# Banded attention and a four-expert layer on one core: dummy products, mask load, weight fetches and the pacing of x operands changed together

## The chip, the cores and the metric

The kernel runs on one core of one Trainium2 chip. The metric is the device time of one execution in microseconds (us). The kernel before has a median of 854.83 us over three runs (854.17 to 855.73).

## The reference, cut to what matters

Everything is float32. Four batches, eight heads, 576 positions, head size 64; then 2304 tokens of width 512, four experts with a hidden width of 1024.

```python
scores = 1/sqrt(64) * q @ k.T                  # per batch and head
mask   = 0 <= rel < 32                         # heads 0..3 (rel = row - column)
mask   = 0 <= rel < 128 and rel % 4 == 0       # heads 4..7
attn   = softmax(where(mask, scores, -1e9)) @ v
x      = attn laid out as [2304, 512]
p      = probs / (sum(probs) + 1e-9)
out    = sum over e of p[:, e] * (relu(x @ w1[e]) @ w2[e])
```

## The kernel before, in words

The host reorders the positions of heads 4 to 7 so that their dilated window becomes a band as well, and pads and transposes q, k and v. On the chip there are two kinds of work.

**Attention** goes by groups of three blocks of 64 queries of one pair of heads: 48 groups, twelve per batch. The first two steps take one group each, every later one two, so there are 25 steps. `attention` (L220) gives eight stages; in iteration n of the loop at L708 stage `s_qk` and `s_max` work on step n, `s_sub` and `s_exp` on step n-1, `s_sum` and `s_norm` on n-2, `s_tr` on n-3 and `s_av` on n-4. TensorE makes the scores (tile `sc`, L264), the transposes (`pt`, L329) and the products with v (`po`, L349); VectorE adds the mask with a running minimum (L278) and sums (L310); GpSimd subtracts and scales (L294, L317); ScalarE takes the exponential (L302) and copies `pt` and `po` out of PSUM (L336, L365). `sc`, `pt` and `po` share four PSUM banks, and an iteration takes five, so the second `sc` of an iteration waits for ScalarE's copy of the same iteration's `po`.

**The experts** run as a generator, `experts` (L500). Every float32 operand is split into a high and a low float32r part, and a product takes three matmuls per 128 rows (`product`, L378). The hidden width is cut into 16 units u, the tokens into three blocks m of 768. A visit (u, m) makes first products of x and w1 (`mm1_a`, L415, and `mm1_b`, L428: seven products in Strassen's manner, two PSUM banks `x` and `y`), then six second products with w2 (`mm2`, L463: each 128 x 512, added into `acc` by VectorE at L488). Block 0 is visited first with every u, blocks 1 and 2 after it; block 0 starts while attention still runs.

**What sets the order.** Each engine works its own list in the order in which the program names the instructions. The loop at L708 issues, per iteration, the loads of q, k and v, the eight stages, some preparations, and then either dummy matmuls (`dummies`, L676: a bfloat16 matmul of 256 columns on a constant, its result read by nobody) or, from START (iteration 10) on, steps of the expert generator: two per iteration up to OPEN (iteration 15), twelve after it (PACE). Preparations (splits of w1, w2 and x, sums of w1 or x quarters) are generators in two lists, `queue` and `later`. `step()` (L569) lets the first of a list do its next piece. After every yield of the experts one piece of `queue` runs, a second if `queue` is longer than 8, and otherwise one of `later` if `queue` is shorter than 5. `later` holds the x operands of blocks 1 and 2 (`x_part`, L208: a ScalarE copy and a subtraction, by VectorE for odd halves i and by GpSimd for even ones; `x_sums`, L198: four VectorE subtractions per half). `need` (L580) runs pieces on the spot until the one wanted is done: at L556 it wants `x_sums` of half 5.

**Loads.** SyncE issues q, k, the mask, the weights and the probabilities; ScalarE issues the v of batches 0 and 1. q, k and v have six buffers each. The program as built deals eight completion counters in turn to the loads of both issuing engines, so a load also waits until the load eight places before it has landed, and what stands behind it on its engine waits with it. The probabilities come in pieces of 16 bytes (L737); w1 and w2 units are 512 KB each.

Of the kernel before, what the change touches and what calls it, by code (L numbers as in the profile page):

```python
# [21 lines left out]
def band_masks(S):  # L22


    import numpy as np

    masks, which = [], []
    for run in (S, S // DILATION):
        for i in range(S // QB):
            a = (i * QB + np.arange(QB))[:, None]  # L30
            c = (i * QB - WINDOW + np.arange(KB))[None, :]
            seen = (c >= 0) & (a - c >= 0) & (a - c < WINDOW) & (a // run == c // run)
            m = np.where(seen, np.float32(0), np.float32(-8e9))
            same = [j for j, other in enumerate(masks) if np.array_equal(other, m)]
            if not same:
                same = [len(masks)]
                masks.append(m)
            which.append(same[0])
    return np.stack(masks), which
# [3 lines left out]
def kernel(  # L43
# [11 lines left out]
    nc = tc.nc  # L55
    _, which = band_masks(qT.shape[3])
    B, NP, _, S = qT.shape
    NT, DM = out.shape
    E, _, F = w1.shape
# [35 lines left out]
    def fetch_w1(u):  # L95
        e, s = divmod(u % NU, FPE)
        r = wp.tile([128, 4, FU], F32, tag="r1", name="r1", bufs=2)
        nc.sync.dma_start(
            out=r, in_=w1[e, :, s * FU:(s + 1) * FU].rearrange("(c p) f -> p c f", p=128)
        )  # L100
        raw1[u] = r

    def fetch_w2(u):
        e, s = divmod(u % NU, FPE)
        r = wp.tile([128, 2, DM], F32, tag="r2", name="r2")
        nc.sync.dma_start(
            out=r, in_=w2[e, s * FU:(s + 1) * FU, :].rearrange("(c p) d -> p c d", p=128)
        )
        raw2[u] = r
# [110 lines left out]
    def attention(ap, xrp, pa):  # L220
        mask = ap.tile(list(masks.shape), F32, name="mask", bufs=1)
# [143 lines left out]
                nc.scalar.activation(out=dst, in_=src, func=AF.Copy)  # L365

        def load_masks():
            nc.sync.dma_start(out=mask, in_=masks)


        stages = (
# [1 line left out]
            (s_qk, 0), (s_max, 0),  # L373
        )
        return chunk, load_masks, load_qk, load_v, stages


# [85 lines left out]
    def mm2(k, first, last, half):  # L463
        u, m = k
        e = u // FPE % E
        if first and m not in acc_t:
            if m == NBL - 1:
                pools["late"]()
            acc_t[m] = pools["acc"].tile([128, TB // 128, DM], F32, name=f"acc_{m}")
        for i in range(TH // 128):  # L470
            at = half * (TH // 128) + i
            tt = m * (TB // 128) + at
            acc = acc_t[m][:, at, :]
            po = pools["m2"].tile([128, 512], F32, tag="m2", name="m2")

            cs = range(2) if half == 0 else (1, 0)
            for n, (c, low) in enumerate([(c, low) for low in range(2) for c in cs]):
                h = h_t[k, f"{c + 1}{half + 1}"][low][:, i * 128:(i + 1) * 128]
                for x, w in enumerate(w2_op[u, c][:2 - low]):
                    nc.tensor.matmul(  # L480
                        po, h, w, start=(n == 0 and x == 0), stop=(n == 3)
                    )
            if first:
                nc.vector.tensor_scalar(
                    out=acc, in0=po, scalar1=pn[:, tt, e:e + 1], scalar2=None, op0=ALU.mult
                )
            else:
                nc.vector.scalar_tensor_tensor(  # L488
                    out=acc, in0=po, scalar=pn[:, tt, e:e + 1], in1=acc,
                    op0=ALU.mult, op1=ALU.add,  # L490
                )
            if last:
                nc.sync.dma_start(out=out[tt * 128:(tt + 1) * 128, :], in_=acc)
            yield


    visits = [(u, 0) for u in range(1, NU)]
# [2 lines left out]
    def experts(begin):  # L500
# [24 lines left out]
        for i, (u, m) in enumerate(visits):  # L525
# [22 lines left out]
            if m == blocks[0]:  # L548
                need(w2_late, u)
            yield from mm2((u, m), *ends, 1)  # L550
            if i + 1 < len(visits):
                begin()
                yield from opening
                if visits[i + 1] == (NU - 1, 0):

                    need(x_sums, 5)  # L556
                    for n in ("T2", "T1"):
                        for j in (4, 5):
                            prepare(x_part, j, n)
            yield from mm2((u, m), *ends, 0)  # L560
            if m == blocks[-1] and u + 2 <= LAST:
                prepare(w2_late, u + 2)
# [3 lines left out]
    queue = []  # L566
    later = []

    def step(of=None):  # L569
        of = queue if of is None else of  # L570
        while of:
            if next(of[0][1], 0) != 0:
                return
            of.pop(0)

    def prepare(what, *args, soon=False, of=None):
        of = queue if of is None else of
        of.insert(0 if soon else len(of), ((what, args), what(*args)))
# [11 lines left out]
    with tc.manual_schedule():  # L590
# [58 lines left out]
        def weigh():  # L649

            nc.vector.reduce_sum(out=ps_, in_=pw, axis=mybir.AxisListType.X)
            nc.vector.tensor_scalar(
                out=ps_, in0=ps_, scalar1=1e-9, scalar2=None, op0=ALU.add
            )
            nc.vector.reciprocal(out=pr_, in_=ps_)
            nc.vector.tensor_tensor(
                out=pn, in0=pw, in1=pr_.to_broadcast([128, NTT, E]), op=ALU.mult
            )
# [17 lines left out]
        def dummies(n):  # L676

            for _ in range(n):
                wt = pools["m2"].tile([128, 512], F32, tag="m2", name="wt")
                nc.tensor.matmul(wt[:, :256], warm[:, :128], warm, start=True, stop=True)  # L680
# [21 lines left out]
        flat = [g for s in steps for g in s]  # L702
        first_x = []
        qk_done = av_done = qk_next = v_next = 0

        dummies(18)
        ffn = experts(begin)
        for n in range(len(steps) + LAG):  # L708
            while qk_next < min(qk_done + min(6, 3 + n), len(flat)):
                load_qk(*flat[qk_next])  # L710
                if qk_next == 0:
                    load_masks()
                qk_next += 1
            while v_next < min(av_done + 6, qk_done + 2, len(flat)):
                load_v(*flat[v_next])
                v_next += 1
            for stage, lag in stages:
                if 0 <= n - lag < len(steps):
                    stage(n - lag, steps[n - lag])
            if n < len(steps):  # L720
                qk_done += len(steps[n])
            if n >= LAG:
                av_done += len(steps[n - LAG])
            for i, names in when.get(n, ()):
                for name in names:
                    of = first_x if i < 2 else later
                    if name is None or name == "T2":
                        prepare(x_sums, i, of=of)
                    if name is not None:
                        prepare(x_part, i, name.upper(), of=of)  # L730
            queue[:0] = first_x
            first_x.clear()
            if n == 3:
                fetch_w1(0)
            if n == 4:
                fetch_w2(0)
                nc.sync.dma_start(out=pw, in_=probs.rearrange("(t p) e -> p t e", p=128))  # L737
            if n == 5:
                prepare(w1_split, 0)
            if n == 7:  # L740
                prepare(w2_late, 0)
                fetch_w1(1)
            if n == START + 1:
                weigh()
                prepare(w1_split, 1)
                prepare(w1_sums, 1)
            if n == OPEN - 1:
                prepare(w2_late, 1)
            if n == START + 2:
                fetch_w2(1)  # L750
            if n == OPEN:
                fetch_w1(2)
            if n == OPEN:
                gate.add("open")
            if n < START:
                dummies(4 if n < 4 else 1)
                step()
                if n > 4:
                    step()
                    step()  # L760
                continue
            for _ in range(PACE if "open" in gate else 2):
                if next(ffn) == "idle":
                    dummies(2)
                    for _ in range(3):
                        step()
                    break
                step()
                if len(queue) > 8:
                    step()  # L770
                elif later and len(queue) < 5:
                    step(later)
        gate.add("over")
        for _ in ffn:
            step()
            if len(queue) > 6:
                step()
            step(later)


# [53 lines left out]
```

## Time and profile before

| what | value |
|---|---|
| median of three runs | 854.83 us |
| the profiled execution | 850.82 us |
| its span, first to last instruction | 849.0 us |
| TensorE busy | 828.1 us, 98% of the span |
| chain that ended last: TensorE's share | 92% |
| VectorE, GpSimd, ScalarE busy | 499.9, 419.1, 327.6 us |
| mean granted TensorE clock | 0.994 |
| loads of k, of v by ScalarE, of the probabilities: issue to landing | 3.3, 4.1, 5.9 us |

The busy times say how long an engine worked in all, not when. Times inside the execution are counted from the first instruction. L numbers are lines of the kernel.

### The profile page before, as it was taken

What the parts mean: (1) busy time and instruction counts of PE and PEld (TensorE: products, weight loads), DVE (VectorE), ACT (ScalarE), POOL (GpSimd) and SP (SyncE); (2) the same over time, 40 slices, a digit from 0 to 9 for tenths busy, and PEclk for the clock granted to TensorE, in tenths of its full rate; (3) what the DMA queues carried; (4) which work ended last, traced back from release to release, by engine and by line L of the source; (5) the groups of instructions that cost most, each with busy time, mean ns of one, the idle gap of its engine ahead of it and who ended that gap; (6) DMA issues with size and microseconds to landing.
All of it is one profiled execution on the core that took longest, in us unless ns stands there. A gap on an engine that the chain in (4) does not pass through costs nothing.

```text
span 849.0 us, 13445 instructions
## 1 busy us (share of the span) xinstructions
PE 828.1 (98%) x5090; PEld 732.1 (86%) x5090; DVE 499.9 (59%) x1027; ACT 327.6 (39%) x772; POOL 419.1 (49%) x484
## 2 busy tenths in 40 slices
PE   8798999999999999999999999999999999999998
PEld 5577788887898888899899898898998998988986
DVE  4777766669555568655545545555555455455554
ACT  3555454445454355533233233242242242232321
POOL 4677987677676678931432332342341342242210
PEclk9999999999999999999999999999999999999999
DMA  8762322332221222310100100101101001010003
GB/s 234 218 184 73 128 85 84 108 120 64 78 90 51 57 71 72 124 51 26 50 25 25 51 26 26 50 25 38 37 26 50 26 25 49 26 35 17 1 26 124
DMA packets 54528, 56.77 MB, mean 67 GB/s; under 512 B 5952, under 2 KB 43840, under 8 KB 54464
## 3 DMA queue, kind: packets, MB, share of 16 engines
q1 hardware_dynamic: 49472, 52.38, 19.9%
q10 hardware_dynamic: 4992, 3.54, 1.5%
q8 instruction: 40, 0.66, 0.3%
q14 instruction: 24, 0.20, 0.1%
HBM read 51.19 MB, written 4.72 MB: 66 GB/s over the span
## 4 chain that ended last, share of the span: by engine, by line
PE 92%; DVE 3%; DMA 1%; ACT 1%; POOL 1%; issue 1%; SPq 0%; ACTq 0%; POOLq 0%; DVEq 0%
PE m L480 45%; PE m1x L382 24%; PE m1y L382 17%; PE po L349 2%; PE sc L264 2%; PE pt L329 2%; DMA q_s<-qT 1%; PE wt L680 1%; DVE acc L488 1%; DMA k_s<-kT 1%; DVE xl_T L116 1%; DVE hl L406 0%; ACT hh L400 0%; DVE xr L203 0%; DVE s L423 0%
## 5 line engine op out<-in xcount | busy, mean ns | idle before, releaser
L488 DVE SCALAR_TENSOR_TENSOR acc<-m,pn,acc 128x512 f32<-128x512 f32 x270 | 201.9, 749 | 130.9 <-PE m L480 130.7
L480 PE MATMUL m<-w2h,hh 128*128 128x512 f32 x576 | 226.9, 394 | 3.9 <-DVE acc L488 3.2
L480 PE MATMUL m<-w2l,hh 128*128 128x512 f32 x576 | 225.4, 391 | 0.0
L116 POOL TENSOR_TENSOR g2l<-r,g2h 128x256 fp32r<-128x256 f32 x124 | 93.0, 775 | 239.7 <-PE m L480 212.2
L480 PE MATMUL m<-w2h,hl 128*128 128x512 f32 x576 | 178.5, 391 | 0.0
L400 ACT ACTIVATE hh<-s 128x384 fp32r<-128x384 f32 x94 | 49.4, 526 | 248.3 <-DVE s L423 197.8
L480 PEld LDWEIGHTS m<-w2h,hh 128*128 128x128 f32 x576 | 108.1, 188 | 26.8 <-DVE acc L488 6.1
L480 PEld LDWEIGHTS m<-w2h,hl 128*128 128x128 f32 x576 | 108.1, 188 | 24.0 <-DVE hl L406 0.3
L480 PEld LDWEIGHTS m<-w2l,hh 128*128 128x128 f32 x576 | 108.2, 188 | 20.1
L116 POOL TENSOR_TENSOR w2l<-r,w2h 128x512 fp32r<-128x512 f32 x62 | 80.6, 1320 | 45.4 <-ACT w2h L113 45.0
L116 POOL TENSOR_TENSOR g1l<-r,g1h 128x256 fp32r<-128x256 f32 x93 | 68.5, 752 | 66.9 <-ACT g1h L113 66.9
L439 DVE TENSOR_TENSOR s<-m1x,s 128x384 f32<-128x384 f32 x47 | 26.2, 557 | 103.0 <-PE m1x L382 101.3
L432 ACT ACTIVATE u<-m1x 128x384 f32<-128x384 f32 x47 | 23.1, 492 | 144.4 <-PE m1x L382 144.4
L406 DVE SCALAR_TENSOR_TENSOR hl<-s,hh 128x384 fp32r<-128x384 f32 x94 | 60.2, 640 | 28.4 <-ACT hh L400 28.4
L382 PE MATMUL m1x<-xh_T,g2h 128*128 128x384 f32 x156 | 53.1, 340 | 1.8 <-DVE s L423 1.8
L382 PE MATMUL m1x<-xl_T,g2h 128*128 128x384 f32 x156 | 52.9, 339 | 0.0
L382 PE MATMUL m1x<-xh_T,g2l 128*128 128x384 f32 x156 | 52.7, 338 | 0.0
L113 ACT ACTIVATE g2h<-r 128x256 fp32r<-128x256 f32 x125 | 43.4, 405 | 4.4 <-POOL r L145 4.4
L382 PE MATMUL m1y<-xl_B,g2h 128*128 128x384 f32 x128 | 43.0, 336 | 0.0
L382 PE MATMUL m1y<-xh_B,g2h 128*128 128x384 f32 x128 | 43.0, 336 | 0.0
L382 PE MATMUL m1y<-xh_B,g2l 128*128 128x384 f32 x128 | 42.9, 335 | 0.0
L278 DVE CUSTOM_DVE_ANT_0 sm<-sc,mask 128x96 f32<-128x96 f32 x144 | 27.8, 254 | 18.8 <-PE sc L264 17.4
(92 smaller groups left out, 1542.3 us busy)
## 6 DMA issues: line engine op xcount, KB each, us to landing
r<-w SPq DMA_DIRECT2D x64, 512.0 KB, 3.5
k_s<-kT SPq DMA_DIRECT2D x48, 112.0 KB, 3.3
q_s<-qT SPq DMA_DIRECT2D x48, 96.0 KB, 3.4
out<-acc SPq DMA_DIRECT2D x18, 256.0 KB, 2.0
v_s<-vw ACTq DMA_DIRECT2D x24, 144.0 KB, 4.1
v_s<-vw SPq DMA_DIRECT2D x24, 144.0 KB, 3.2
mask<-masks SPq DMA_DIRECT2D x1, 288.0 KB, 4.6
pw<-probs SPq DMA_DIRECT2D x1, 36.0 KB, 5.9
```

Of the source, the lines that this page charges most:

```text
L113: nc.scalar.activation(out=hi, in_=src, func=AF.Copy)
L116: lo_eng.tensor_tensor(out=lo, in0=src, in1=hi.bitcast(F32), op=ALU.subtract)
L264: nc.tensor.matmul(banks[swap][o, i * KB:(i + 1) * KB], q_s[h, c0:c0 + QB], k_s[h, c0:c0 + KB], start=True, stop=True, skip_group_check=True,)
L278: nc.vector.tensor_tensor_reduce(out=sm[:, k * GB + i, :KB], in0=banks[k][:, i * KB:(i + 1) * KB], in1=mask[:, which[blk if p < NP // 2 el ...
L329: nc.tensor.transpose(pt[:KB, i * 128:(i + 1) * 128], sm[:, k * GB + i, :KB], ident)
L382: nc.tensor.matmul(bank, w[:, k], x[:, k], start=(first and k == 0 and i == 0), stop=(last and k == 1 and i == 2), skip_group_check=True,)
L400: nc.scalar.activation(out=hi, in_=src, func=AF.Relu)
L406: nc.vector.scalar_tensor_tensor(out=lo, in0=src, scalar=0.0, in1=hi.bitcast(F32), op0=ALU.max, op1=ALU.subtract)
L432: nc.scalar.activation(out=u2, in_=x, func=AF.Copy)
L439: nc.vector.tensor_tensor(out=s5, in0=x, in1=s5, op=ALU.add)
L480: nc.tensor.matmul(po, h, w, start=(n == 0 and x == 0), stop=(n == 3))
L488: nc.vector.scalar_tensor_tensor(out=acc, in0=po, scalar=pn[:, tt, e:e + 1], in1=acc, op0=ALU.mult, op1=ALU.add,)
```

## The change

- Up to START every iteration issues four dummy matmuls; before, four in iterations 0 to 3 and one in 4 to 9.
- The mask is loaded by two DMAs of ScalarE (patterns 0 and 1; patterns 2 to 5), ahead of the first q and k; before, by one DMA of SyncE behind the first q and k.
- The loads of q and k run six groups ahead from the start (no `3 + n`).
- The first w2 unit and the probabilities are fetched in iteration 6 (before: 4), the second w1 unit in 8 (before: 7); the split of the first w2 unit is queued in 8 (before: 7).
- `mm2` yields "acc", and no piece of `later` runs after such a yield; after the other yields one runs if `queue` is shorter than 8 (before: 5, after any yield). Behind the loop a piece of `later` ran after every yield, now after every yield that isn't "acc".

```diff
         def load_masks():
-            nc.sync.dma_start(out=mask, in_=masks)
+            nc.scalar.dma_start(out=mask[:, :2], in_=masks[:, :2])
+            nc.scalar.dma_start(out=mask[:, 2:], in_=masks[:, 2:])
@@ mm2
                 nc.sync.dma_start(out=out[tt * 128:(tt + 1) * 128, :], in_=acc)
-            yield
+            yield "acc"
@@ the loop
-            while qk_next < min(qk_done + min(6, 3 + n), len(flat)):
-                load_qk(*flat[qk_next])
+            while qk_next < min(qk_done + 6, len(flat)):
                 if qk_next == 0:
                     load_masks()
+                load_qk(*flat[qk_next])
                 qk_next += 1
...
-            if n == 4:
+            if n == 6:
                 fetch_w2(0)
                 nc.sync.dma_start(out=pw, in_=probs.rearrange("(t p) e -> p t e", p=128))
             if n == 5:
                 prepare(w1_split, 0)
-            if n == 7:
+            if n == 8:
                 prepare(w2_late, 0)
                 fetch_w1(1)
...
             if n < START:
-                dummies(4 if n < 4 else 1)
+                dummies(4)
                 step()
...
             for _ in range(PACE if "open" in gate else 2):
-                if next(ffn) == "idle":
+                at = next(ffn)
+                if at == "idle":
...
                 step()
                 if len(queue) > 8:
                     step()
-                elif later and len(queue) < 5:
+                elif at != "acc" and len(queue) < 8:
+
                     step(later)
         gate.add("over")
-        for _ in ffn:
+        for at in ffn:
             step()
             if len(queue) > 6:
                 step()
-            step(later)
+            if at != "acc":
+                step(later)
```

## Rows read from the trace of the kernel before

**Rows 1.** The page: busy us of each engine, share of span, instructions.

```profile
PE 828.1 (98%) x5090; PEld 732.1 (86%) x5090; DVE 499.9 (59%) x1027; ACT 327.6 (39%) x772; POOL 419.1 (49%) x484
```

**Rows 2.** Busy by stretch: PE, PEld, DVE, ACT, POOL, granted clock, DMA share, GB/s.

```profile
10.00:20.00 10.00, 8.04 (x137) 5.81 (x138) 5.76 (x41) 4.57 (x11) 6.21 (x7) 0.83 0.90 262
...
450.00:500.00 50.00, 50.00 (x251) 45.19 (x250) 26.19 (x42) 14.79 (x34) 13.47 (x18) 1.00 0.10 33
```

**Rows 3.** Timeline of ScalarE: start, us, instruction, [idle before, releaser].

```profile
25.85 1.24 ACTq L252 DMA_DIRECT2D v_s<-vw  x2
27.14 0.55 ACT L365 ACTIVATE xr<-po 128x192 f32<-128x192 f32 x2 [3.95 <-issue]
...
36.30 0.69 ACT L365 ACTIVATE xr<-po 128x192 f32<-128x192 f32 x2 [2.40 <-DMA k_s<-kT]
```

**Rows 4.** Timeline of SyncE's queue around the weight loads.

```profile
17.49 0.47 SPq L737 DMA_DIRECT2D pw<-probs  x1
18.93 3.61 SPq L245 DMA_DIRECT2D q_s<-qT  x1
22.59 0.43 SPq L246 DMA_DIRECT2D k_s<-kT  x1
...
29.05 0.38 SPq L98 DMA_DIRECT2D r<-w  x1
```

**Rows 5.** Timeline of TensorE up to the first expert product: dummies (L680) and waits.

```profile
11.36 0.72 PE L680 MATMUL wt<-ident 128*128 128x256 bf16 x4
13.89 0.73 PE L349 MATMUL po<-pts,v_s 96*64 96x64 f32 x12 [1.81 <-ACT pts L336]
...
19.11 0.28 PE L680 MATMUL wt<-ident 128*128 128x256 bf16 x1
...
27.75 1.22 PE L264 MATMUL sc<-k_s,q_s 64*64 64x96 f32 x20 [1.40 <-ACT xr L365]
...
40.26 0.45 PE L382 MATMUL m1x<-xh_B,g1h 128*128 128x384 f32 x1
```

**Rows 6.** Stretches of TensorE alone: busy, granted clock, DMA share, GB/s.

```profile
15.00:17.00 2.00, 2.00 (x30) 0.50 0.98 317
...
29.00:31.00 2.00, 2.00 (x27) 0.50 0.92 253
```

**Rows 7.** Timeline of TensorE where block operands x are made.

```profile
93.07 0.39 PE L480 MATMUL m<-w2h,hh 128*128 128x512 f32 x1
...
97.89 0.50 PE L480 MATMUL m<-w2h,hh 128*128 128x512 f32 x1 [1.89 <-DVE acc L488]
...
211.75 0.50 PE L480 MATMUL m<-w2h,hh 128*128 128x512 f32 x1 [1.27 <-DVE acc L488]
...
320.82 0.44 PE L382 MATMUL m1x<-xh_T,g1h 128*128 128x384 f32 x1 [0.50 <-DVE s L439]
...
328.21 0.39 PE L480 MATMUL m<-w2h,hh 128*128 128x512 f32 x1
...
336.51 0.34 PE L382 MATMUL m1x<-xh_T,g1h 128*128 128x384 f32 x1
```

**Rows 8.** Timeline of VectorE in the same places.

```profile
93.54 0.55 DVE L423 TENSOR_TENSOR s<-m1x,s 128x384 f32<-128x384 f32 x1
...
325.01 1.63 DVE L203 TENSOR_TENSOR xr<-xr 128x384 f32<-128x384 f32 x2
...
330.84 0.55 DVE L423 TENSOR_TENSOR s<-m1x,s 128x384 f32<-128x384 f32 x1
331.98 0.56 DVE L406 SCALAR_TENSOR_TENSOR hl<-s,hh 128x384 fp32r<-128x384 f32 x1 [0.59 <-ACT hh L400]
...
333.48 2.06 DVE L488 SCALAR_TENSOR_TENSOR acc<-m,pn,acc 128x512 f32<-128x512 f32 x3
```

**Rows 9.** The x sums (L203), 319 to 334 us: ns min/median/max.

```profile
L203 DVE TENSOR_TENSOR xr<-xr x8: 544/982/1100, 320.7 to 332.5; 128x384 f32<-128x384 f32 x8
```

**Rows 10.** Timeline of GpSimd beside the sums.

```profile
332.33 2.52 POOL L116 TENSOR_TENSOR g2l<-r,g2h 128x256 fp32r<-128x256 f32 x3 [1.94 <-ACT g2h L113]
```

## The prediction, made before the changed kernel was run

> **What bounds the kernel now.** I read the busy times first, then the stretches, then the waits of TensorE, and then the timelines of the engines at the places where it waits. TensorE is busy for 828.1 of 849.0 us [rows 1]; in a late stretch, 450 to 500 us, it has no idle time at all (50.00 of 50.00) while VectorE is at half load and DMA at a tenth [rows 2]. No edit can give anything there. All the idle time is 21 us, and the last add and store at the end, which are not touched, are part of it. So the change can act in two places: ahead of START (the first expert product is at 40.26 us [rows 5]), where TensorE is busy for 8.04 of the 10 us from 10 to 20, at 0.83 of its clock, and DMA for 0.90 [rows 2], and at the few waits of TensorE between 90 and 340 us, where the x operands of blocks 1 and 2 are made [rows 7].
>
> Ahead of START the last wait of an iteration is mostly ScalarE's. It sat for 3.95 us before its copy at 27.14 [rows 3]. It had to issue two loads of v there, and the first went out only at 25.85, because its counter belonged to a load of k issued at 22.59 [rows 4] (a k lands in 3.3 us). That k was late because the q before it took 3.61 us to issue, straight behind the probabilities, which come in 16-byte pieces [rows 4]. TensorE paid with 1.40 us of idling at 27.75 [rows 5] and, after it, two microseconds at half clock [rows 6]. At 36.30 ScalarE waits again, 2.40 us [rows 3], behind loads that had queued after the second w1 unit, issued at 29.05 [rows 4].
>
> **The change part by part.** The sum is made against the profiled execution's own 850.82 us (span 849.0 and 1.82 around it). That execution is 4.0 us below the median of 854.83, so I carry the difference over, not the time.
>
> *Mask and the six groups ahead: 0.* SyncE's list of q and k keeps its order; it loses one issue of some 0.5 us, ScalarE gains two ahead of its first v loads. Cover: the first scores stand behind the eighteen dummies at the beginning, and ScalarE's first exponential behind scores, minimum and subtraction. If a v must wait for a counter on ScalarE, or a q comes earlier, the ends are +0.5 and -0.5 us (one issue).
>
> *Weights and probabilities later: -2.0.* The q and k of groups 12 to 15 no longer stand behind w2 and the probabilities, so ScalarE's first v at 25.85 finds its counter free: the 1.40 us of idling go. Two of the probabilities' successors change places, though. The burst of 16-byte pieces now blocks the q of group 16 and later ones, which are needed two steps after; I take it that this slack hides it. The second w1 unit moves behind two more groups: of the 2.40 us at 36.30, 1.24 are ScalarE's own two issues [rows 3] and stay, 1.16 are waiting, and I count half, 0.6. Sum -2.0. Ends: 0, if the burst only makes the same stall one or two iterations later, and -3.6, if both waits go (2.56) and the two microseconds at half clock [rows 6] with them (1.0).
>
> *Eighteen more dummies: +1.0.* Four in place of one cost 0.72 - 0.28 = 0.44 us in an iteration at full clock [rows 5], and at half clock at most twice that, 0.88. They come behind the scores, and TensorE's next work is `po`, for which ScalarE must have copied `pt`. Where ScalarE ends the wait they fall into idle time. I see two iterations without this cover: 4, at half clock [rows 6], where TensorE runs without a gap from 13.89 us on [rows 5], so that the later scores delay VectorE's minimum, the w1 splits queued behind it and then the normalising for `pt` (0.6, between the two), and 9, whose dummies stand directly ahead of START (0.44). Ends: 0 and 0.88 + 5 x 0.44 = 3.1.
>
> On the clock the trace says this: at 15 to 17 us it stood at 0.50, the 1.2 GHz level [rows 6], after TensorE had idled for 1.81 us behind the dummies of iteration 3, four of them, which ended at 12.1 [rows 5]. So four dummies did not hold it there, and I count no gain. The Trainium skill ("TensorE: Matmul & The Clock Gate", What's actually happening) says that activity releases the throttle; by that rule eighteen more could keep the clock up. It is a rival below.
>
> *x operands of block 1: -0.8.* I walked the two lists by the code's rules. For half 2, before, the sums stood ahead of and between the second products' adds, and TensorE waited 1.89 us for an add at 97.89 [rows 7]. After, three of the four sums run at first products. The subtraction that began at 93.54 behind a sum [rows 8] can begin when its product ends, 93.07 [rows 7], 0.47 earlier; one sum stays ahead of the first add. I count 0.5; ends 0 and 1.89. For half 3 the wait of 1.27 us at 211.75 [rows 7] came from subtractions between adds. They move to first products, but three sums now come just ahead of an earlier visit's adds. I count 0.3; ends -1.27 and +1.3 (the same wait at another place).
>
> *x operands of block 2: +1.2.* Here the list comes out worse. The eight sums were spread one by one over the eight yields that end where the experts call `need(x_sums, 5)`. Now the x parts wait for first products, only one sum is done one yield before, and `need` runs seven on the spot: between the first product that ends at 328.21 [rows 7] and three adds. On VectorE: subtraction and `hl` take until 1.70 us after the product's end (331.98 + 0.56 - 330.84 [rows 8]), 329.9; seven sums at the 0.82 of the pair that ran back to back here (1.63 for two [rows 8]) 5.7, 335.6; three adds 2.06 [rows 8], 337.7; then the subtraction that frees bank x for its last product, 0.55, 338.2. TensorE wants that bank at 336.51 [rows 7]. So it waits 1.7 us, and the 0.50 at 320.82 [rows 7], which an x part in the way caused, goes: +1.2. Ends, with sums of 0.544 and 0.982 [rows 9]: 336.3, no wait, -0.5; 339.3, a wait of 2.8, +2.3.
>
> Sum: -2.0 + 1.0 - 0.8 + 1.2 = -0.6, that is 850.2 in an execution like the profiled one, and 854.2 against the median. I call the bound of what can be told from no change 0.2%, 1.7 us: 853.1 to 856.5.
>
> **The rivals.**
>
> *Both early waits go, and the dummies are hidden.* -3.6 and nothing for the dummies, x of block 1 as above (-0.8), block 2 even (0): -4.4, 850.4. For it: DMA has little left to carry between the bursts, and ScalarE ends most waits. Against it: DMA is 0.90 busy from 10 to 20 us [rows 2], so that the waits may be the bytes' own.
>
> *The dummies hold the clock.* The stretches of 15 to 17 and 29 to 31 us at full clock would save 2 x 1.0 us [rows 6], and the dummies of iteration 4 would cost 0.44 instead of 0.6; with the forecast's other terms, 854.2 - 2.2 = 852.0. Against it: the row after iteration 3's dummies.
>
> *The burst only moves.* The stall of iteration 7 comes back in 8, where a v's counter now belongs to a load of this burst. The -2.0 is lost: 856.2.
>
> *The seven sums cost more: slower.* Place: the pass before 336.51. GpSimd works beside them with subtractions of 0.84 us (2.52 for three [rows 10]), and the sums take 0.544 at the least and 0.982 in the middle [rows 9], so most of them wait for something. If in the burst every sum waits out a whole GpSimd instruction, 7 x (0.544 + 0.84) = 9.7 us in place of 5.7: a wait of 5.7 us in place of 1.7, +4.0, 858.2. It decides from a mean of 0.57 us per sum on, where TensorE begins to wait, and the change as a whole is slower than the bound from 1.2 us per sum on. The Trainium skill ("SBUF — State Buffer", Who interferes with whom) states such an exclusive port pair between VectorE and GpSimd. By that rule the second one to start blocks fully, which would give the 858.2; the sums' spread agrees with blocking, and their middle stands half way.
>
> *Nothing at START.* If the product at 40.26 is held by the arrival of its x, all early terms fall away and 855.2 is left; this is inside the forecast.
>
> **How the numbers follow.** Forecast 0.40, with a range of its own of 852.7 to 855.7; both early waits 0.20; the clock 0.10; the burst that moves 0.12; the costly sums 0.18. Faster (below 853.1): 0.20 from both waits, 0.09 from the clock and 0.06 from the forecast's edge, 0.35. Slower (above 856.5): 0.16 from the costly sums and 0.04 from the edges of the moved burst and the forecast, 0.20. Same: 0.45. For 8 in 10 I take the time from 850.3 to 858.2, between the first rival and the last.
>
> **What would show it.** In the trace after: ScalarE's two v loads of iteration 7 follow its split without a gap, and the first expert product is at 39 to 39.5 us (above 40.3: the burst moved or the dummies cost; below 37.5: the first rival). The clock between 14 and 31 us. The wait for an add near 97 us at 1.4 us. Seven sums in a row on VectorE some 290 us after START, and behind them a wait of TensorE for `s` (L439) of 1 to 3 us. The prediction is wrong if START moves by more than 2.5 us, or if no wait follows the seven sums.

## The result, and the profile after

The changed kernel takes 862.70 us (median of 6 runs, 860.40 to 864.49); the kernel before, beside it, 855.28 (853.98 to 856.06). The ratio is 1.0085, 95% interval 1.0068 to 1.0102: 5.8 to 8.7 us slower. The forecast of 854.2 and its range up to 858.2 were wrong. The profiled execution took 863.16 us, span 861.4. It stands near its median, while that of the kernel before lies 4 us under its own, so the two profiles differ by more than the kernels do.

TensorE's line of the page shows 835.1 us busy for 828.1, and 26.3 us without work for 20.9 [rows 1]:

```profile
PE 835.1 (97%) x5108; PEld 736.6 (86%) x5108; DVE 503.3 (58%) x1027; ACT 327.4 (38%) x772; POOL 417.5 (48%) x484
```

Eighteen more instructions are the dummies, some 3.2 us at the 0.72 for four of [rows 5]; the rest of the longer busy time I put down to products at a lower clock (0.986 in the mean for 0.994). The stretches (busy of PE, PEld, DVE, ACT and POOL, granted clock, DMA share, GB/s) show the late part unchanged [rows 2], and 30 to 40 us at a clock of 0.66 (0.94 before):

```profile
10.00:20.00 10.00, 8.12 (x123) 5.38 (x122) 5.55 (x40) 4.73 (x11) 6.27 (x7) 0.83 0.93 262
30.00:40.00 10.00, 8.00 (x110) 6.15 (x111) 5.97 (x30) 6.15 (x16) 5.17 (x6) 0.66 0.76 219
...
450.00:500.00 50.00, 50.00 (x249) 44.99 (x248) 26.86 (x43) 15.84 (x36) 18.24 (x22) 1.00 0.14 42
```

**Ahead of START.** The burst of 16-byte pieces moved, and its wait with it. On SyncE's queue a q again takes 3.47 us to issue behind the probabilities, 3.61 before [rows 4]:

```profile
22.71 0.44 SPq L106 DMA_DIRECT2D r<-w  x1
23.19 0.64 SPq L738 DMA_DIRECT2D pw<-probs  x1
23.93 3.47 SPq L245 DMA_DIRECT2D q_s<-qT  x1
```

ScalarE's two v loads go out late behind it, in iteration 8 where it was 7, and its copy waits 3.27 us for that q where it waited 3.95 [rows 3]:

```profile
29.54 1.81 ACTq L252 DMA_DIRECT2D v_s<-vw  x2
31.40 0.55 ACT L365 ACTIVATE xr<-po 128x192 f32<-128x192 f32 x2 [3.27 <-DMA q_s<-qT]
```

TensorE's timeline: the scores of iteration 7 follow without a gap, as forecast, those of iteration 8 wait 2.65 us, and the first expert product is at 41.01 for 40.26 [rows 5]. That difference can't be told from the spread of single executions: in the profiles of the six kernels with all the early edits as here, this one among them, the product starts at 39.45 to 42.00 us, 40.9 in the mean, and in those of the five without any, at 40.26 to 41.57, 40.8 in the mean.

```profile
26.02 0.73 PE L264 MATMUL sc<-k_s,q_s 64*64 64x96 f32 x24
...
32.00 1.22 PE L264 MATMUL sc<-k_s,q_s 64*64 64x96 f32 x20 [2.65 <-ACT xr L365]
...
41.01 0.44 PE L383 MATMUL m1x<-xh_B,g1h 128*128 128x384 f32 x1
```

**Block 1.** These are the x operands of block 1 (halves 2 and 3, as those of block 2 are 4 and 5). Half 2's wait of 1.89 us is 1.47, as forecast (1.4). Half 3's single wait of 1.27 [rows 7] has become four, 4.35 us in all:

```profile
99.93 0.50 PE L481 MATMUL m<-w2h,hh 128*128 128x512 f32 x1 [1.47 <-DVE acc L489]
...
200.09 0.45 PE L383 MATMUL m1x<-xh_T,g1h 128*128 128x384 f32 x1 [0.62 <-DVE s L440]
207.54 0.50 PE L481 MATMUL m<-w2h,hh 128*128 128x512 f32 x1 [2.32 <-DVE acc L489]
217.79 0.50 PE L481 MATMUL m<-w2h,hh 128*128 128x512 f32 x1 [0.79 <-DVE acc L489]
224.25 0.45 PE L383 MATMUL m1x<-xh_T,g1h 128*128 128x384 f32 x1 [0.62 <-DVE s L440]
```

The two of 0.62 come behind x subtractions of 0.78 us (L116) that now run at first products, the other two behind sums (L203). VectorE's timeline shows what stands ahead of the longest. Three sums run at the last first products of a visit, and the visit's adds come behind them:

```profile
202.51 1.09 DVE L203 TENSOR_TENSOR xr<-xr 128x384 f32<-128x384 f32 x1
203.52 0.55 DVE L407 SCALAR_TENSOR_TENSOR hl<-m1x,hh 128x384 fp32r<-128x384 f32 x1
203.99 2.84 DVE L203 TENSOR_TENSOR xr<-xr 128x384 f32<-128x384 f32 x2
206.75 1.40 DVE L489 SCALAR_TENSOR_TENSOR acc<-m,pn,acc 128x512 f32<-128x512 f32 x2
```

GpSimd's timeline beside the two sums:

```profile
203.59 2.83 POOL L116 TENSOR_TENSOR w2l<-r,w2h 128x512 fp32r<-128x512 f32 x2 [0.40 <-ACT w2h L113]
```

Before, only single x subtractions of some 0.98 us stood between the adds there. Now two sums of 1.42 each end at 206.83; the add follows, and TensorE, which wants the bank, starts at 207.54.

**Block 2.** The seven sums stand in a row, as forecast, but take 7.15 us, 1.02 each, where I took 0.82:

```profile
335.68 0.93 DVE L407 SCALAR_TENSOR_TENSOR hl<-s,hh 128x384 fp32r<-128x384 f32 x1 [0.59 <-ACT hh L401]
336.53 7.15 DVE L203 TENSOR_TENSOR xr<-xr 128x384 f32<-128x384 f32 x7
343.60 2.06 DVE L489 SCALAR_TENSOR_TENSOR acc<-m,pn,acc 128x512 f32<-128x512 f32 x3
345.58 0.54 DVE L440 TENSOR_TENSOR s<-m1x,s 128x384 f32<-128x384 f32 x1
```

GpSimd's timeline beside them has seven subtractions without a gap, 6.86 us:

```profile
335.45 3.78 POOL L116 TENSOR_TENSOR g2l<-r,g2h 128x256 fp32r<-128x256 f32 x4
339.19 3.08 POOL L116 TENSOR_TENSOR g1l<-r,g1h 128x256 fp32r<-128x256 f32 x3
```

TensorE waits 3.45 us for `s`, in place of the 0.50 at 320.82 [rows 7]:

```profile
342.39 0.34 PE L383 MATMUL m1y<-xl_B,g2h 128*128 128x384 f32 x1
346.18 0.69 PE L383 MATMUL m1x<-xh_T,g1h 128*128 128x384 f32 x1 [3.45 <-DVE s L440]
```

and then runs at half clock, as TensorE's stretches show (busy, clock, DMA share, GB/s); at 0.50, the 1.2 GHz level, half of 1.82, 2.00 and most of the next 2.00 us is lost, some 2.8 us:

```profile
344.00:346.00 2.00, 0.00 (x0) 0.76 0.00 0
346.00:348.00 2.00, 1.82 (x6) 0.50 0.00 0
348.00:350.00 2.00, 2.00 (x8) 0.50 0.03 8
350.00:352.00 2.00, 2.00 (x7) 0.53 0.00 0
352.00:354.00 2.00, 2.00 (x11) 1.00 0.00 0
```

### The profile page after: what moved, and what is told of

It reads as the page before. It is cut to its first block, busy times and chain, and to the rows that moved or that the text cites. A ratio compares the mean times of both kernels' runs of the same rounds, so it can differ in the third digit from the quotient of the medians.

```text
span 861.4 us, 13467 instructions
## 1 busy us (share of the span) xinstructions
PE 835.1 (97%) x5108; PEld 736.6 (86%) x5108; DVE 503.3 (58%) x1027; ACT 327.4 (38%) x772; POOL 417.5 (48%) x484
## 4 chain that ended last, share of the span: by engine, by line
PE 89%; DVE 5%; ACT 2%; POOL 1%; DMA 1%; issue 1%; SPq 0%; ACTq 0%; DVEq 0%; POOLq 0%
PE m L481 44%; PE m1x L383 23%; PE m1y L383 16%; PE po L349 2%; DVE xr L203 2%; PE sc L264 2%; PE pt L329 2%; PE wt L681 1%; DVE hl L407 1%; DMA pw<-probs 1%; DVE acc L489 1%; ACT hh L401 0%; DVE sm L278 0%; DMA q_s<-qT 0%; ACT xh_T L113 0%
## 5 line engine op out<-in xcount | busy, mean ns | idle before, releaser
L116 POOL TENSOR_TENSOR g2l<-r,g2h 128x256 fp32r<-128x256 f32 x124 | 92.7, 776 | 239.6 <-PE m L481 213.3
L116 POOL TENSOR_TENSOR g1l<-r,g1h 128x256 fp32r<-128x256 f32 x93 | 69.1, 762 | 72.4 <-ACT g1h L113 72.3
L116 POOL TENSOR_TENSOR w2l<-r,w2h 128x512 fp32r<-128x512 f32 x62 | 80.0, 1312 | 46.1 <-ACT w2h L113 45.8
```

Source lines behind the costliest of these rows:

```text
L116: lo_eng.tensor_tensor(out=lo, in0=src, in1=hi.bitcast(F32), op=ALU.subtract)
```

## The experiments

Each was timed in five rounds against the kernel before. Every execution also lists its span and mean granted clock. From these I split a time in two: (1 - clock) x span is what the clock took, and clock x span is the rest (products and idle time at full clock). The split has a limit: a low clock counts in it also while TensorE waits (0.76 at 344 to 346 us above, without a product), where it costs nothing. Behind the loop, where TensorE hardly waits otherwise, that is half a microsecond; ahead of START, where TensorE works for 31.3 of the first 40 us before, the split can't tell a gain from a wait that grew. Means over all executions of a kernel, in us:

| kernel | median | ratio to before [95%] | clock x span | taken by the clock |
|---|---|---|---|---|
| before (81 runs on three chips) | 854.7 to 855.2 | 1 | 844.0 | 9.0 |
| changed | 862.7 | 1.0085 [1.0068, 1.0102] | 850.6 | 10.0 |
| e1 pacing alone | 864.1 | 1.0107 [1.0079, 1.0136] | 849.9 | 12.5 |
| e2 early edits alone | 854.0 | 0.9989 [0.9974, 1.0004] | 845.6 | 6.6 |
| e3 sums spread again | 856.7 | 1.0022 [1.0007, 1.0037] | 848.5 | 6.6 |
| e4 wait filled | 860.5 | 1.0061 [1.0038, 1.0084] | 850.9 | 7.6 |
| e5 dummies alone | 855.0 | 0.9998 [0.9982, 1.0014] | 846.5 | 6.7 |
| e6 weights alone | 855.2 | 1.0002 [0.9985, 1.0019] | 844.2 | 9.2 |
| e7 sums on GpSimd | 865.6 | 1.0118 [1.0099, 1.0137] | 852.4 | 10.9 |
| e8 early edits, wider pieces | 852.5 | 0.9972 [0.9958, 0.9986] | 844.9 | 5.6 |
| e9 pacing in the loop alone | 857.5 | 1.0032 [1.0016, 1.0048] | 847.0 | 8.9 |
| e10 pacing behind the loop alone | 860.2 | 1.0058 [1.0036, 1.0080] | 847.2 | 11.3 |
| e11 e10, wait filled | 858.3 | 1.0037 [1.0019, 1.0054] | 847.6 | 9.1 |
| e12 GpSimd idle beside the sums | 857.4 | 1.0030 [1.0012, 1.0048] | 849.1 | 6.9 |

"Before" differs by at most 0.6 us between the three chips in either column. The other means are over six executions (changed, e1, e4, e7, e10) or twelve, with standard errors of 0.3 to 1.0 us, so I read differences of under 1 us as none, and a single one of up to 2 us as uncertain.

My theory was: the loss is VectorE's, from the x sums that the pacing bunches up, in two places, and the early edits cancel. The rival for the place was that the early edits lose the time (the burst of small pieces moved, dummies in the way); the rival for the cause of the slow sums was that they need 1 us by themselves.

**e1 and e2: which half.** The kernel before with the pacing of the x parts alone (the "acc" yields in both loops), and with all the rest alone (mask, six ahead, weights, dummies).

```diff
 e1
-            yield
+            yield "acc"
...
-                elif later and len(queue) < 5:
+                elif at != "acc" and len(queue) < 8:
...
+            if at != "acc":
+                step(later)
 e2
+            nc.scalar.dma_start(out=mask[:, :2], in_=masks[:, :2])
...
-            if n == 4:
+            if n == 6:
...
-                dummies(4 if n < 4 else 1)
+                dummies(4)
...
```

> The kernel before with the pacing edits alone (the acc yields, the looser bound on the queue, and no later piece after acc behind the loop); mask, weights and dummies as before. Theory P, the pacing costs the time: in the profile after, seven x sums of block 2 run in a row (7.15 us), TensorE waits 3.45 us for the subtraction behind them and runs some 5 us at half clock, and half 3 costs two more waits, so this kernel is 5 to 8 us slower than before. Rival Q, the early edits cost it (later start, dummies, loads): within 2 us of before.

> The kernel before with the early edits alone (mask by ScalarE in two parts, six groups ahead, w2 and probabilities in iteration 6, second w1 in 8, four dummies up to START); the pacing as before. Theory P: 0 to 2 us over before, first expert product at about 41 us in place of 40.3. Rival Q: 5 to 8 us over before.

The whole loss is in e1; e2 is within the bound, -1.0 us. e1's trace repeats the four waits of half 3 (0.62, 2.32, 0.79, 0.62) and the wait behind the sums (3.42), but in that execution, the fastest of e1's six, the clock stayed up behind it, as TensorE's stretches show:

```profile
344.00:346.00 2.00, 0.00 (x1) 1.00 0.00 0
346.00:348.00 2.00, 2.00 (x11) 1.00 0.00 0
348.00:350.00 2.00, 2.00 (x11) 1.00 0.04 8
```

In e10 (below), with the same wait of 3.42, it fell to 0.50 again. So the fall of the clock is a matter of the execution. The table gives its mean: 12.5 us against 9.0.

**e3: the sums behind the loop spread again.** The changed kernel, with a piece after every yield behind the loop.

```diff
-            if at != "acc":
-                step(later)
+            step(later)
```

> The changed kernel, but behind the loop a later piece runs after every yield as before, so that the eight sums of block 2 are spread again; the main loop keeps the new pacing. Theory P: the 3.45 us wait and the half clock behind it go, 4 to 6 us faster than the changed kernel, 1 to 3 over before. Rival Q: as slow as the changed kernel, 6 to 8 us over before.

856.7 us: 6 us of the 7.4 are back. The wait behind the sums is the 0.50 of before; half 3 keeps its four. By the columns, 2.1 of it at full clock and 3.4 by the clock.

**e9 and e10: the two places by themselves.** The kernel before with the pacing in the loop alone, and behind the loop alone.

```diff
 e9
...
-                elif later and len(queue) < 5:
+                elif at != "acc" and len(queue) < 8:
...
 e10
...
-            step(later)
+            if at != "acc":
+                step(later)
```

> The kernel before with the pacing of the loop alone: 'acc' yields skipped, later pieces at queue < 8; behind the loop a piece after every yield, as before. Theory (the loss of the pacing has two places, each with its own wait of TensorE): half 3 shows the four waits .62, 2.32, .79, .62 (4.35 us) near 200 to 225 us in place of 1.27, the time is 2.5 to 3.5 us above before (+0.3 to 0.4%), and no seven sums stand in a row near 330 us. Rival (the loss is all in the burst of seven sums): within 0.5 us of before.

> The kernel before with the pacing behind the loop alone. Theory: the seven sums stand in a row (7.1 us), TensorE waits 3.4 us for s behind them, half 3 has its 1.27 us alone; the time is 3 us above before where the clock holds and 5.5 us above it where TensorE runs at half clock behind the wait (0.35 to 0.65%). Rival (all loss is in the loop): within 0.5 us of before.

e9: +3.0 us at full clock; its waits in half 3 exceed those of before by 4.35 - 1.27 = 3.1. e10: +3.2 at full clock, for waits of 3.42 - 0.50 = 2.9, and +2.3 by the clock. The two add up to 6.2 at full clock, e1 has 5.9, and the waits account for both.

By the column e9 pays nothing to the clock (8.9 for 9.0), but its profile shows a price. TensorE's stretches of e9 and, below it, of the kernel before:

```profile
180.00:235.00 55.00, 50.59 (x363) 0.97 0.23 73
...
180.00:235.00 55.00, 53.66 (x389) 1.00 0.28 84
```

Behind the wait of 2.32 the products of e9 run at 0.50 and then 0.65 for 2 us each, which loses 1.7 us. Six of the seven profiles with this wait show such a fall, of 1.5 to 1.7 us (e4's does not); no profile without it does. Part of it may come back at half 2: behind its wait of 1.85 to 1.90 us the clock fell in two of seven profiles (e6, e10), behind the 1.43 to 1.49 of the new pacing in none of seven. What the loop's pacing costs by the clock, between nothing and these 1.7 us, stays open; the ratio bounds what it costs in all, 2.7 us [1.4, 4.1].

**e4 and e11: the wait filled.** The changed kernel and e10, each with 28 dummies on TensorE where it waits behind the sums.

```diff
         product(y, u, "S4", m, "B22", False)
+        if k == (NU - 1, 0):
+            wt = pools["m2"].tile([128, 512], F32, tag="m2", name="wt")
+            for _ in range(28):
+                nc.tensor.matmul(wt[:, :256], pools["warm"][:, :128], pools["warm"], start=True, stop=True)
...
```

> The changed kernel with 28 dummy matmuls (about 3 us at full clock) put into the place where TensorE waits for the subtraction behind the seven sums. If the half clock after that wait (2.6 us lost) is the idling's, it goes: 2 to 3 us faster than the changed kernel, 4 to 6 over before. If the clock would fall anyway, or the dummies delay work: 7 us over before or more. Rival Q: no change, 7 over before.

> The kernel of the pacing behind the loop alone, with 28 dummy products on TensorE where it waits behind the seven sums (they take 3.2 us at full clock). Theory (wait and clock are two prices): the wait's 3 us stay, the clock stays at 1.00, and the time is 0 to 2.5 us under the kernel without the dummies, 3 us above before. Rival (the clock costs nothing in most executions): the two kernels are equal within 0.5 us.

In e11's timeline of TensorE the dummies leave 0.35 us of the wait:

```profile
339.38 3.23 PE L445 MATMUL wt<-ident 128*128 128x256 bf16 x28
...
342.96 0.44 PE L382 MATMUL m1x<-xh_T,g1h 128*128 128x384 f32 x1 [0.35 <-DVE s L439]
```

The clock stands at 1.00 in the stretches behind, in both. In e11 and e4 clock x span stays (+0.4 and +0.3) and the clock's part falls by 2.2 and 2.4. The intervals of the ratios overlap with those of the kernels without the fill, so the ratios alone would leave it open; two pairs with the same difference, in the column where it must be, say that wait and clock are two prices (each difference has a standard error of 0.9 us, the two together 0.6).

**e12: why a sum takes 1.02 us.** The changed kernel with GpSimd's work beside the sums left out: seven w1 subtractions are copies on ScalarE, and four w1 sums fall away.

```diff
...
+        if u == NU:
+            return
...
-            split(gh[v], gl[v], r[v], nc.scalar, nc.gpsimd)
+            if u == NU - 1:
+                nc.scalar.activation(out=gh[v], in_=r[v], func=AF.Copy)
+                nc.scalar.activation(out=gl[v], in_=r[v], func=AF.Copy)
+            else:
+                split(gh[v], gl[v], r[v], nc.scalar, nc.gpsimd)
```

> The changed kernel with GpSimd's work beside the seven sums left out: the low parts of w1 for one unit's late operands (four subtractions) and the next unit's first ones (three) are copies on ScalarE, and the four w1 sums of that unit are left out; all else as in the changed kernel. Theory (VectorE's sums are held up by GpSimd's instructions beside them): the seven sums take 0.54 to 0.60 us each, 3.8 to 4.2 us in place of 7.15, TensorE's wait for s behind them falls from 3.45 to under 0.8 us, and the time is 3 to 5 us under that of the changed kernel. Rival (a sum with two operands in these buffers takes 1.0 us by itself): the seven still take 7 us, the wait and the time stay as they are.

The timelines of VectorE, TensorE and GpSimd, which has nothing to do beside the sums:

```profile
335.25 4.06 DVE L213 TENSOR_TENSOR xr<-xr 128x384 f32<-128x384 f32 x7
339.23 2.06 DVE L499 SCALAR_TENSOR_TENSOR acc<-m,pn,acc 128x512 f32<-128x512 f32 x3
...
342.35 0.44 PE L393 MATMUL m1x<-xh_T,g1h 128*128 128x384 f32 x1 [0.27 <-DVE s L450]
...
340.39 1.01 POOL L116 TENSOR_TENSOR xl_B<-xr,xh_B 128x384 fp32r<-128x384 f32 x1 [5.83 <-ACT xh_B L113]
```

0.58 us per sum for 1.02, a wait of 0.27 for 3.45, and a time at e3's (the intervals overlap). The sums of block 2 were slow because of GpSimd; those of half 3 were not tried this way. Later in e12, beside VectorE's adds, a GpSimd subtraction of these takes 0.71, and it takes the same with VectorE idle (1.41 for two in e7, below):

```profile
347.36 2.84 POOL L116 TENSOR_TENSOR g2l<-r,g2h 128x256 fp32r<-128x256 f32 x4
```

Beside the sums it took 3.78 for four, 0.95: both engines pay. The Trainium skill ("SBUF — State Buffer", Who interferes with whom) says that a VectorE instruction with two SBUF inputs contends with a GpSimd instruction that reads SBUF, and calls what they share an exclusive lock. The traces agree on who contends: 1.02 us per sum beside GpSimd's subtractions, 0.58 without. Taking full turns, seven sums and seven subtractions would need 7 x (0.58 + 0.71) = 9.0 us; they took 7.15, so here the turns overlap in part.

**e7: the sums on GpSimd.** The changed kernel with block 2's sums on GpSimd, to take them out of VectorE's way.

```diff
-            nc.vector.tensor_tensor(
+            (nc.gpsimd if i > 3 else nc.vector).tensor_tensor(
```

> The changed kernel with the eight x sums of block 2 on GpSimd, everything else as changed. If VectorE's list is what TensorE waits for (seven sums in front of three adds and the subtraction), the 3.45 us wait goes whatever GpSimd needs for the sums, 4 to 6 us faster than the changed kernel, about 2 over before. If the sums' result itself is what is late (the x operands of block 2), the wait stays or grows: 7 us over before or more.

A miss, and the slowest of all. TensorE no longer waits for VectorE, but for a w1 split that now stands behind the sums on GpSimd:

```profile
339.14 7.38 POOL L203 TENSOR_TENSOR xr<-xr 128x384 f32<-128x384 f32 x7
346.48 1.41 POOL L116 TENSOR_TENSOR g2l<-r,g2h 128x256 fp32r<-128x256 f32 x2
...
347.26 0.69 PE L383 MATMUL m1x<-xh_T,g2l 128*128 128x384 f32 x1 [5.22 <-POOL g2l L116]
```

A burst of seven costs on either engine when work that TensorE needs stands behind it.

**e5 and e6: the early edits apart.** The kernel before with the dummies alone, and with the later weights alone.

```diff
 e5
-                dummies(4 if n < 4 else 1)
+                dummies(4)
 e6
-            if n == 4:
+            if n == 6:
...
-            if n == 7:
+            if n == 8:
```

> The kernel before with four dummies in every iteration up to START, nothing else. As predicted: +1.0 us (0 to 3.1), the first expert product at 41 to 42 us. Rival: the dummies fall into idle time, no change within 1 us. Other rival, they hold the clock: 1 to 2 us faster, and no stretch at 0.5 between 14 and 31 us.

> The kernel before with the first w2 unit and the probabilities fetched in iteration 6 and the second w1 unit in 8, nothing else. As predicted: -2.0 us. The profile after says otherwise, the wait moved from iteration 7 to 8 (TensorE waits 2.65 us at 32.0 for ScalarE in place of 1.40 at 27.75): then 0 to +1 us, first expert product at 40 to 41.5 us.

Neither moves the time. In e5 the clock takes 2.3 us less and the rest is 2.5 us longer; in its trace 20 to 30 us is at 1.00 where it was 0.89, but 10 to 20 stays at 0.83, 40 to 44 is at 0.50 and 0.73, and the first expert product, at 43.22 us, is the latest of all profiles. Whether the two columns are a gain and a cost isn't shown: dummies that only hold the clock up while TensorE waits for others would move time from one to the other in the same way and change nothing. e6 changes neither column: the wait of iteration 7 is gone, and iteration 8 has it.

```profile
30.69 1.23 PE L264 MATMUL sc<-k_s,q_s 64*64 64x96 f32 x20 [2.69 <-ACT xr L365]
```

**e8: the burst made shorter.** The early edits (e2), with the probabilities stored partition by partition in DRAM, so that they come in pieces of 288 bytes.

```diff
-                nc.sync.dma_start(out=pw, in_=probs.rearrange("(t p) e -> p t e", p=128))
+                nc.sync.dma_start(out=pw, in_=probs)
...
-        "probs": moe_domain_probs[rows],
+        "probs": moe_domain_probs[rows].reshape(-1, 128, E).transpose(1, 0, 2),
```

> The early edits alone, and the probabilities laid out so that each partition's 72 numbers are one piece (128 pieces of 288 bytes in place of 2304 of 16). If the burst of small pieces blocks SyncE and through the counters ScalarE, the 3.5 us issue behind the probabilities shrinks below 1 us, TensorE's wait for ScalarE in iteration 8 (2.5 to 4 us) goes, and the kernel is 1.5 to 3 us faster than the early edits alone, which were 1 us faster than before. Rival, the bytes themselves are the bound: the wait stays within 0.5 us and the time is that of the early edits alone.

The q behind the probabilities issues in 1.24 us, for 3.32 in e2 and 3.47 in the changed kernel. ScalarE's wait stays, 3.19 for 3.67 in e2:

```profile
29.23 0.55 ACT L365 ACTIVATE xr<-po 128x192 f32<-128x192 f32 x2 [3.19 <-DMA q_s<-qT]
```

So the small pieces alone were not what held that q. What did (the w2 unit ahead of it, or its own issue order) was not tried. The kernel is the fastest of all: 852.5 us, 0.28% under before [0.14 to 0.42%]. Against e2 (854.0) the intervals overlap.

## Why the prediction was wrong

*Mask and six ahead (0):* no run had it by itself. By the ratios e2 is at -1.0 us, e5 at -0.2 and e6 at +0.2, which leaves -1.0 for it. Each of the three is known to 1.2 to 1.5 us, so the term stays open.

*Weights later (-2.0):* failed. The rival "the burst only moves" came true: e6 is at 0 in both columns. I had seen the rival's mechanism and gave the slack of two steps more weight. What waited was not the scores that use the late q, but ScalarE's v loads, one iteration on.

*Eighteen dummies (+1.0):* measured -0.2 [-1.5, +1.2] (e5). The granted clock does rise with them: in the mean it takes 2.3 us less of the span. I had dismissed that rival on one row, the wait behind iteration 3's dummies; that stretch is at 0.83 in e5 too, and the clock was higher between 20 and 30 us. The Trainium skill's rule ("TensorE: Matmul & The Clock Gate", What's actually happening), that activity releases the throttle, was the better guide to the clock there. The rival's 2 us of time did not come: either the dummies cost as much elsewhere (whom they delay was not tried), or a higher clock is worth little where TensorE waits.

*Early edits together (-1.0):* measured -1.0 [-2.2, +0.3]. That is luck: the -2.0 and the +1.0 that make it up both came out near nothing.

*x of block 1 (-0.8):* half 2 right (1.47 for 1.4). Half 3, -0.3, failed: it was +3.1 in waits (e9: +3.0 at full clock), beyond my end of +1.3. I had seen that three sums come ahead of adds, and priced them as the old wait at a new place. There are four waits: 2.32 and 0.79 behind sums, which take 1.0 to 1.4 us each beside GpSimd's instructions, and twice 0.62 behind x subtractions held for first products. And behind the longest the clock fell in most profiles, for which I had no term.

*x of block 2 (+1.2):* the step that failed most. The place, the seven in a row and the waiting product were right, and so was the walk: with 1.02 for 0.82 it gives 329.9 + 7.15 + 2.06 + 0.55 = 339.7, a wait of 3.2 (3.45 measured), just above my upper end of 2.8. I took 0.82 from a pair, although the middle of the eight was 0.98 [rows 9], with GpSimd beside them then too. And the wait's second price is missing: behind it TensorE ran at half clock in some executions, 2.3 us in the mean in e10 and 3.4 in the comparison of e3 with the changed kernel. That such a wait is followed by half clock was to be read in my own rows, at 15 to 17 and 29 to 31 us [rows 5, 6]. Instead of +1.2, the term is +2.1 to +3.2 and 2.3 to 3.4.

*The sum:* early -1.0, loop +3.0, behind the loop +5.0 to +6.0, together +7 to +8; measured +7.4. The rival "the seven sums cost more" had the mechanism and the sign, a chance of 0.18, and too small a price, because it had neither the clock nor half 3. Its 5.7 us of wait were too many by themselves.

## What to carry to other kernels

Work that an engine does in the gaps is cheap because it is spread. Before you hold it back, find the point that needs it all: there it comes in one piece, at the speed it has beside the other engines, ahead of whatever is queued behind. A wait of TensorE has two prices, the wait and the clock after it; read both from the kernel's own rows. Dummies give back the second, not the first.

## What the runs showed that I had not expected

- Whether the clock falls behind the same wait differs by execution: 3.42 us at 1.00 afterwards in e1, 3.45 us at 0.50 in the changed kernel. So it does behind the 2.32 of half 3: six profiles of seven. One profile can't price it; the mean clock of all executions can, to about 1 us, where TensorE doesn't wait otherwise.
- GpSimd slows too: 0.95 us for 0.71 beside VectorE's sums.
- Moving the weights changed which iteration pays, at the same price: 1.40 us in iteration 7 before, 2.69 in iteration 8 in e6, and no change of the time.
